# Hash attention and a gated feed-forward layer on one core: hash products, sums and casts placed anew

## The chip, the cores and the metric

The kernel runs on one core of a Trainium2 chip. The core has five engines, each with its own in-order queue of instructions: TensorE (PE, matrix products), VectorE (DVE), ScalarE (ACT), GpSimd (POOL) and SyncE (SP, which here issues transfers only). They wait for each other through semaphores. Transfers run on 16 DMA engines that all queues share. The metric is the time of one execution on the device in microseconds; the figure shown for a kernel is the median of several runs.

## The reference

Inputs are q, k and v of shape 4 batches x 8 heads x 768 tokens x 64, a random matrix `proj` of 64 x 6, and four weight matrices. All are float32.

```python
q_bits = (einsum('bhsd,dk->bhsk', q, proj) > 0)      # 6 bits, likewise k_bits
q_bucket = sum(q_bits * 2 ** arange(6))               # likewise k_bucket
scores = where(q_bucket == k_bucket, q @ k.T / 8, -1e9)
attn = softmax(scores) @ v
x = attn.transpose(0, 2, 1, 3).reshape(3072, 512)
ffn = (gelu(x @ w_gate) * (x @ w_val)) @ w_out         # d_ff = 1536
out = x + sigmoid(x @ w_res) * ffn
```

A token attends only to tokens of the same bucket, that is, to those whose six signs agree. The kernel does not build a mask: it appends the six bits (as plus or minus a half, with a constant) to the 64 values of q and k, scaled so that a score with unequal bits falls far below the others.

## The kernel before

Batches are numbered 0 to 3. A batch has 4 pairs of heads (pair p = 4 b + hp), each pair has 9 score chunks, so a batch has 36 slots; slot `s` of batch `b` is number `36 b + s` in the code. For every pair q and k must be brought into the form `aug`: cast to bf16 (`cast`, lines 259 to 263) into a tile `nat`, given their hash bits, and transposed, by a DMA transpose on SP (`turn`, line 359). There are four `nat` tiles, used in turn.

Each batch goes through three kinds of stage:

- Attention: in each slot TensorE computes one chunk of scores (line 499), ScalarE takes the exp (line 509), and two slots later TensorE multiplies with v (line 474). VectorE resets (`opened`, line 441), copies (`repeat`, line 453) and normalises (`finish`, lines 418 and 419) the accumulators `av`; there are two of them. The normalised rows are transposed into `x_sb` by SP (line 427). Between the chunks TensorE works off the second half of the feed-forward layer of the batch before (`project`, lines 555 and 569).
- Gate: for 12 steps m, TensorE multiplies x with a block of the gate weights and of the value weights (line 523), ScalarE takes the gelu of the first (line 540), VectorE multiplies the two (`hh`, line 543). Two PSUM tiles `sp` alternate, so the step after needs the gelu and the product of the step before.
- Project of the last batch, at the end.

The order of batch 0 and of its gate stage is written out by hand in `PLAN` and `BESIDE_GV`. For later batches, work is hung on slots with `at` and on gate steps with `gv`; what hangs on a slot or step is issued after its own work, in the order in which it was hung there.

The hash bits come about in two ways. For two pairs of a batch TensorE multiplies (line 282, ahead of gate step 1), and VectorE takes the signs in four small instructions for each of the four tiles (line 303, in gate steps 0, 1, 2 and 4). For the other two pairs of batches 2 and 3 (pairs 10, 11 and 14, 15) the work is spread out: for each of the four tiles there are 12 products of GpSimd (`product`, line 334), of half a tile with one column of `proj`, and 12 sums of VectorE over the 64 values (`add_up`, line 340). So batch b's attention, its gate stage and the attention of batch b + 1 together carry 48 products and 48 sums, for b = 1 and 2. `PLACES[b]` names the place of each product: `('a', b, s)` is slot s of batch b, `('g', b, m)` is gate step m. The products of attention slots use two buffers of the tag `gt`, which they share with the gelu's output; those of gate steps use two buffers of the tag `th`, shared with `project`. A product waits until its buffer is free, that is, until the sum two products before is done. Sums are not placed by themselves: `spread_out` issues one ahead of a product when two products are outstanding in its list, and the rest at a change of tag or at `DRAIN`. `LAYS` is where GpSimd turns the finished sums into bits (line 343) and SP transposes. `LDY` is where the tiles of these pairs are loaded, `CSY` at which gate step and on which engine they are cast; `LDX`, `TRX` and `CSX` are the first slots of the loads, VectorE's transposes (line 271) and GpSimd's casts of the other two pairs.

`load_rows` (line 350) loads the 384 numbers of `proj` to all 128 partitions, with a transfer on GpSimd's queue, and `spread_rows` (line 354) reorders them into the tile that all products read. GpSimd also prepares v for each pair (`vals_s` and `vals_a`, lines 385 to 397, a block of six instructions).

SP's queue is in order too: a transfer or a transpose that waits for its data holds up all behind it.

Of the kernel before, what the change touches and what calls it, by code (L numbers as in the profile page):

```python
# [9 lines left out]
FP32 = mybir.dt.float32  # L10
# [45 lines left out]
    ('turn_dma', 3, 0),  # L56
# [27 lines left out]
    (1, 'tokens', (6, 7), True), (4, 'cast', 6, 0, 'p'), (5, 'cast', 6, 1, 'p'), (7, 'cast', 7, 0, 'p'),  # L84
    (6, 'cast', 7, 1, 'p'), (7, 'bits', 6, 0, 'v'), (7, 'turn_dma', 6, 0), (10, 'bits', 6, 1, 'v'),
    (10, 'turn_dma', 6, 1), (9, 'bits', 7, 0, 'v'), (9, 'turn_dma', 7, 0), (10, 'bits', 7, 1, 'v'),
    (10, 'turn_dma', 7, 1), (9, 'ps'),
]
XDMA = 2
XJOIN = (1, 2)  # L90
# [3 lines left out]
def kernel(  # L94
# [13 lines left out]
    B, H, S, D = q.shape  # L108
    NBITS = proj.shape[1]
    DMODEL = H * D  # L110
    DFF = moe_w_gate.shape[1]
    P = 128
# [9 lines left out]

    LDX, TRX, CSX = 9, 24, 25
    LDY = {1: [('a', 1, 0), ('a', 1, 0), ('a', 1, 2), ('a', 1, 3)], 2: [('a', 2, 0), ('a', 2, 1), ('a', 2, 16), ('a', 2, 17)]}
    CSY = [(5, 's'), (6, 's'), (7, 's'), (8, 's')]
    PLACES = {1: [('a', 1, 11), ('a', 1, 12), ('a', 1, 13), ('a', 1, 14), ('a', 1, 15), ('a', 1, 16), ('a', 1, 17), ('a', 1, 18), ('a', 1, 21), ('a', 1, 22), ('a', 1, 23), ('a', 1, 24), ('a', 1, 25), ('a', 1, 26), ('a', 1, 31), ('a', 1, 32), ('g', 1, 0), ('g', 1, 0), ('g', 1, 1), ('g', 1, 1), ('g', 1, 2), ('g', 1, 2), ('g', 1, 3), ('g', 1, 3), ('g', 1, 4), ('g', 1, 4), ('g', 1, 5), ('g', 1, 5), ('g', 1, 6), ('g', 1, 6), ('g', 1, 7), ('g', 1, 7), ('g', 1, 8), ('g', 1, 8), ('g', 1, 9), ('g', 1, 9), ('g', 1, 10), ('g', 1, 10), ('a', 2, 2), ('a', 2, 3), ('a', 2, 4), ('a', 2, 5), ('a', 2, 6), ('a', 2, 7), ('a', 2, 8), ('a', 2, 9), ('a', 2, 12), ('a', 2, 13)], 2: [('a', 2, 14), ('a', 2, 15), ('a', 2, 16), ('a', 2, 17), ('a', 2, 18), ('a', 2, 21), ('a', 2, 22), ('a', 2, 23), ('a', 2, 24), ('a', 2, 25), ('a', 2, 26), ('a', 2, 31), ('a', 2, 32), ('g', 2, 0), ('g', 2, 0), ('g', 2, 1), ('g', 2, 1), ('g', 2, 2), ('g', 2, 2), ('g', 2, 3), ('g', 2, 3), ('g', 2, 4), ('g', 2, 4), ('g', 2, 5), ('g', 2, 5), ('g', 2, 6), ('g', 2, 6), ('g', 2, 7), ('g', 2, 7), ('g', 2, 8), ('g', 2, 8), ('g', 2, 9), ('g', 2, 9), ('g', 2, 10), ('g', 2, 10), ('a', 3, 2), ('a', 3, 3), ('a', 3, 4), ('a', 3, 5), ('a', 3, 6), ('a', 3, 7), ('a', 3, 8), ('a', 3, 9), ('a', 3, 12), ('a', 3, 13), ('a', 3, 14), ('a', 3, 15), ('a', 3, 16)]}
    DRAIN = {1: ('a', 2, 15), 2: ('a', 3, 18)}
    LAYS = {1: [('g', 1, 6), ('g', 1, 7), ('g', 1, 11), ('a', 2, 16)], 2: [('g', 2, 6), ('g', 2, 7), ('a', 3, 5), ('a', 3, 19)]}  # L130
    NE = 9
    C = 2048.0
    ALPHA = C / np.sqrt(D)
# [6 lines left out]
    g_pool = ctx.enter_context(tc.tile_pool(name="gtmp", bufs=2))  # L140
# [126 lines left out]
    def tr(p, side, c0=0, c1=HT):  # L267
        if (p, side) not in t32:
            t32[p, side] = t32_pool.tile([P, HT, 2, 32], FP32, tag="t32", name="t32")
        sl = slice(c0, c1)  # L270
        nc.vector.transpose(t32[p, side][:, sl].rearrange("p c h n -> p (c h n)"),  # L271
                            raw[p, side][:, sl].rearrange("p c d -> p (c d)"))
# [56 lines left out]
    def product(x, n, tag):  # L329
        bit, hi = divmod(n, 2)  # L330
        if x not in sums:
            sums[x] = hh_pool.tile([P, HT, NBITS], FP32, tag=f"sums{x[0] % 2}{x[1]}", name="sums")
        pr = g_pool.tile([P, T, D], FP32, tag=tag, name="pr")
        nc.gpsimd.tensor_mul(pr, raw[x][:, hi * T:(hi + 1) * T],  # L334
                             projr[:, bit].unsqueeze(1).to_broadcast([P, T, D]))
        prods.append((x, bit, hi, pr))
# [5 lines left out]
    def bits_sums(x):  # L342
        nc.gpsimd.tensor_scalar(nat_of(x)[:, :, D:D + NBITS], sums.pop(x), 0.0, 0.5,
                                op0=ALU.is_gt, op1=ALU.subtract)

    rows = []

    def load_rows():
        rows.append(g_pool.tile([P, D, NBITS], FP32, tag="th", name="pr"))
        nc.gpsimd.dma_start(rows[0].rearrange("p d n -> p (d n)"),  # L350
                            proj.rearrange("d n -> (d n)").partition_broadcast(P))

# [3 lines left out]
    def turn(p, side):  # L356
        x = (p, side)
        ag = aug_pool.tile([P, HT, P], BF16, tag=f"aug{side}", name=f"aug{side}")
        nc.sync.dma_start_transpose(out=ag, in_=nat_of(x).rearrange("p c n -> p (c n)"))
        aug[x] = ag  # L360
# [94 lines left out]
    def x_turn(b, hp):  # L455
        pt = mm_ps.tile([P, T, P], BF16, tag="f" if b == 0 else "r", name="pt")
        for t in range(T):
            nc.tensor.transpose(pt[:, t, :], x_tok[b][:, hp, t, :], ident)
        if hp == HP - 1:
            nc.scalar.activation(x_sb[b][:, hp, 0:2], pt[:, 0:2], AF.Copy)  # L460
            nc.vector.tensor_copy(x_sb[b][:, hp, 2:T], pt[:, 2:T])
        else:
            nc.vector.tensor_copy(x_sb[b][:, hp], pt)
# [117 lines left out]
    NSLOT = HP * NCH  # L581
# [7 lines left out]
    def at(s, *pieces):  # L589
        side_work.setdefault(s, []).extend(pieces)  # L590
# [4 lines left out]
    def gv(b, m, *pieces):  # L595
        gv_work.setdefault((b, m), []).extend(pieces)

    def loads(s, *xs):
        for p, what in xs:
            at(s, (lambda p=p: load_v(p)) if what == "v" else  # L600
               (lambda p=p, w=what: load(p, "qk".index(w))))
# [15 lines left out]
    def tokens(ps, psum=False):  # L617
        hash_tok([(p, side) for p in ps for side in range(2)], psum)
# [4 lines left out]
    def put(where, b, i, *pieces):  # L623
        if where == "g":
            gv(b, i, *pieces)
        else:
            at(b * NSLOT + i, *pieces)

    def spread_out(ys, places, drain, lays):
        work = [(y, n) for y in ys for n in range(2 * NBITS)]  # L630
        assert len(places) == len(work)
        left, tagged = [], None
        for k, (where, b, i) in enumerate(places):
            tag = "th" if where == "g" else "gt"
            if tagged not in (None, tag):
                for _ in left:
                    put("a", b, 0 if tag == "gt" else NSLOT - 1, add_up)
                left = []
            tagged = tag
            if len(left) > 1:  # L640
                left.pop(0)
                put(where, b, i, add_up)
            y, n = work[k]
            put(where, b, i, lambda y=y, n=n, tag=tag: product(y, n, tag))
            left.append((y, n))
        for _ in left:
            put(*drain, add_up)
        for y, p in zip(ys, lays):
            put(*p, lambda y=y: bits_sums(y), lambda y=y: turn(*y))

    for b in range(B - 1):
        s0, p0 = b * NSLOT, (b + 1) * HP
        xs = [(p0 + i, side) for i in range(2) for side in range(2)]
        ys = [(p0 + 2 + i, side) for i in range(2) for side in range(2)]
        if b == 0:
            continue
        for j, x in enumerate(xs):
            loads(s0 + LDX + 3 * j, (x[0], "qk"[x[1]]))
            at(s0 + TRX + 2 * j, lambda x=x: tr(*x))
            at(s0 + CSX + 2 * j, lambda x=x: cast(*x, nc.gpsimd))  # L660
        gv(b, 0, lambda p0=p0: tokens((p0, p0 + 1), True))
        for m, x in zip((0, 1, 2, 4), xs):
            lay(b, m, x)
        for y, (where, bb, i) in zip(ys, LDY[b]):
            put(where, bb, i, lambda y=y: load(y[0], y[1]))
        for y, (m, eng) in zip(ys, CSY):
            gv(b, m, lambda y=y, eng=eng: cast(*y, ENG[eng]))
        spread_out(ys, PLACES[b], DRAIN[b], LAYS[b])
    for p in range(HP, NPAIR):
        if 9 * p - 8 >= NSLOT:  # L670
            at(9 * p - 8, lambda p=p: vals_s(p), lambda p=p: vals_a(p))
        if 9 * p - 20 >= NSLOT:
            loads(9 * p - 20, (p, "v"))
# [25 lines left out]
    def first_gv(i):  # L699
# [3 lines left out]
        S=score, V=value, fill=fill, tr=tr,  # L703
# [9 lines left out]
        turn_dma=turn,  # L713
        hash=lambda ps, i: hash_mm([(p, side) for p in ps for side in range(2)], (i % 2,), (i // 2,)),
        tokens=tokens, bits=lambda p, side, e: bits(p, side, [ENG[x] for x in e]),
        va=vals_a, vs=vals_s, finish=finish, open=opened, preset=preset, repeat=repeat,
        pr=load_rows, ps=spread_rows, w=load_w, load=load, load_v=load_v, xturn=lambda hp: x_turn(0, hp),
        gelu=gelu_table, gv=first_gv)

    for m, name, *args in BESIDE_GV:  # L720
# [7 lines left out]
    for s in range(NSLOT, LAST):  # L728
# [11 lines left out]
        if slot == NSLOT - 1:  # L740
            values(*pending.pop(0))
            ps = (HP * (b + 1), HP * (b + 1) + 1)
# [47 lines left out]
```

## Time and profile before

| | us |
|---|---|
| median of 3 runs | 342.61 (342.59 to 343.22) |
| profiled execution | 344.1 |
| its span | 342.3 |
| TensorE busy | 331.2 |
| VectorE busy | 215.4 |
| ScalarE busy | 214.2 |
| GpSimd busy | 176.6 |

The span runs from the first to the last instruction that the profiler records; the execution is a little longer. Stages by the profile's clock: attention of batch 0 to about 47 us, its gate stage to 82, attention of batch 1 to 124, gate to 161, batch 2 to 204 and 241, batch 3 to 283 and 318, the last project to the end. In rows of a timeline the columns are start, length, engine, line, operation, output and input, and in brackets the idle time of the engine before it with what ended that. A row with x2 or x4 merges neighbours. In the chain of work that ended last each row is start, length and what held the path.

### The profile page before, as it was taken

Reading aid. Unit: us, or ns where it says so; the run is one execution under the profiler, and the core shown is the slowest. Engines: PE = TensorE matmul, PEld = TensorE weight load, DVE = VectorE, ACT = ScalarE, POOL = GpSimd, SP = SyncE. Lnnn points to the kernel's source line nnn. Section 1 sums busy time; section 2 is a strip of 40 time slices with the busy share of each in tenths; the row PEclk is TensorE's granted clock in tenths of the full one; section 3 lists DMA queues with packets and bytes.
Section 4 is the critical chain, followed back from the end, with each engine's and each line's share of the span. In section 5 each row is a group of like instructions: output and inputs, shape, how many; then the busy total and the mean of one; then the engine's idle time right before and its main releaser. Section 6 shows DMA issues by size and latency. Waiting matters only on the chain.

```text
span 342.3 us, 7607 instructions
## 1 busy us (share of the span) xinstructions
PE 331.2 (97%) x2995; PEld 203.1 (59%) x3042; DVE 215.4 (63%) x454; ACT 214.2 (63%) x247; POOL 176.6 (52%) x264
## 2 busy tenths in 40 slices
PE   8999999999999999999999999999999999999995
PEld 6666665565666655555666565555566665566443
DVE  7977455655467958877577875887477444343333
ACT  4989962237999952355999881254999984223120
POOL 3798940282248942688799971677988100000000
PEclk9999999999999999999999999999999999999998
DMA  7999999999987324434656823624041450000012
GB/s 209 377 255 186 294 180 159 165 171 131 246 295 195 83 74 92 90 72 57 170 180 183 237 75 101 124 47 92 2 125 45 64 101 31 33 0 2 31 71 86
DMA packets 74388, 43.89 MB, mean 128 GB/s; under 512 B 52544, under 2 KB 71360, under 8 KB 74352
## 3 DMA queue, kind: packets, MB, share of 16 engines
q1 hardware_dynamic: 67872, 37.95, 46.5%
q0 software_dynamic: 6400, 5.44, 10.6%
q8 instruction: 24, 0.39, 0.5%
q14 instruction: 12, 0.10, 0.1%
q10 hardware_dynamic: 80, 0.00, 0.0%
HBM read 29.56 MB, written 6.29 MB: 105 GB/s over the span
## 4 chain that ended last, share of the span: by engine, by line
PE 77%; DVE 7%; POOL 6%; DMA 4%; issue 3%; ACT 1%; SPq 1%; DVEq 0%; POOLq 0%; ACTq 0%
PE sp L523 31%; PE fps L569 16%; PE sp L499 14%; PE av L474 8%; PE rps L555 6%; DVE hh L543 3%; PE hs L282 2%; DMA ldv<-in_v_dram 2%; DMA aug<-nat 2%; POOL pr L334 2%; DVE nat L303 2%; DVE sums L340 1%; POOL nat L303 1%; ACT ering L509 1%; POOL va L385 1%
## 5 line engine op out<-in xcount | busy, mean ns | idle before, releaser
L334 POOL TENSOR_TENSOR pr<-ld,projr 128x384 f32<-128x384 f32 x96 | 93.5, 997 | 57.1 <-DVE sums L340 34.3
L509 ACT ACTIVATE e<-sp 128x1024 bf16<-128x1024 f32 x108 | 109.1, 1027 | 8.5 <-PE sp L499 3.4
L540 ACT ACTIVATE gt<-sp 128x768 bf16<-128x768 f32 x48 | 38.9, 810 | 84.7 <-PE sp L523 81.0
L499 PE MATMUL sp<-aug,aug 71*128 71x256 bf16 (+1 forms) x384 | 85.9, 325 | 1.5 <-ACT ering L509 0.6
L569 PE MATMUL fps<-wo,hh 128*128 128x512 bf16 (+2 forms) x287 | 74.4, 361 | 1.3
L543 DVE TENSOR_TENSOR hh<-gt,sp 128x768 bf16<-128x768 bf16 x48 | 45.8, 954 | 42.7 <-PE sp L523 39.2
L523 PE MATMUL sp<-x_sb,wv 128*128 128x512 bf16 (+1 forms) x374 | 70.4, 324 | 2.0 <-DVE hh L543 1.5
L523 PE MATMUL sp<-x_sb,wg 128*128 128x512 bf16 (+1 forms) x377 | 70.6, 325 | 0.4
L340 DVE TENSOR_REDUCE sums<-pr 128x6 f32<-128x384 f32 x96 | 50.0, 541 | 11.8 <-POOL pr L334 11.2
L474 PEld LDWEIGHTS <-e 128*128 128x128 bf16 x864 | 40.2, 97 | 25.1
L523 PEld LDWEIGHTS <-wv 128*128 128x128 bf16 x384 | 37.5, 98 | 27.4 <-issue 2.7
L523 PEld LDWEIGHTS <-wg 128*128 128x128 bf16 x384 | 37.1, 98 | 25.7 <-issue 1.5
L474 PE MATMUL av<-va,e 128*128 128x65 bf16 x864 | 43.4, 193 | 0.2
L569 PEld LDWEIGHTS <-hh 128*128 128x128 bf16 x312 | 28.1, 97 | 21.7
L499 PEld LDWEIGHTS <-aug 71*128 71x128 bf16 x384 | 29.2, 97 | 12.9 <-issue 3.3
L509 ACT ACTIVATE ering<-sp 128x1024 bf16<-128x1024 f32 x36 | 34.3, 1030 | 2.6 <-PE sp L499 2.4
L572 DVE SCALAR_TENSOR_TENSOR fps<-th,fps 128x512 f32<-128x512 f32 (+2 forms) x26 | 17.0, 653 | 28.3 <-PE fps L569 28.3
L555 PE MATMUL rps<-wr,x_sb 128*128 128x512 bf16 x91 | 26.0, 379 | 0.2
L559 ACT ACTIVATE th<-rps 128x512 f32<-128x512 f32 x24 | 14.3, 594 | 18.5 <-PE rps L555 18.5
L271 DVE STREAM_TRANSPOSE t<-ld 128x768 f32<-128x768 f32 (+3 forms) x28 | 23.2, 846 | 3.4 <-PE hs L282 1.9
L453 DVE COPY av<-av 128x390 f32<-128x390 f32 x24 | 13.6, 566 | 13.6 <-PE av L449 13.6
L261 POOL TENSOR_SCALAR nat<-ld 128x768 bf16<-128x768 f32 (+1 forms) x12 | 9.6, 803 | 20.1 <-DMA aug<-nat 16.7
(72 smaller groups left out, 264.6 us busy)
## 6 DMA issues: line engine op xcount, KB each, us to landing
ldv<-in_v_dram SPq DMA_DIRECT2D x16, 384.0 KB, 4.7
out_dram<-o SPq DMA_DIRECT2D x23, 256.0 KB, 2.1
ld<-in_q_dram SPq DMA_DIRECT2D x15, 384.0 KB, 5.2
ld<-in_k_dram SPq DMA_DIRECT2D x15, 384.0 KB, 6.0
wg<-in_moe_w_gate_dram POOLq DMA_DIRECT2D x4, 384.0 KB, 6.5
wv<-in_moe_w_val_dram POOLq DMA_DIRECT2D x4, 384.0 KB, 8.9
wo<-in_moe_w_out_dram POOLq DMA_DIRECT2D x3, 512.0 KB, 6.9
wr<-in_moe_w_res_dram POOLq DMA_DIRECT2D x1, 512.0 KB, 13.8
```

The source lines that it names most:

```text
L271: nc.vector.transpose(t32[p, side][:, sl].rearrange("p c h n -> p (c h n)"), raw[p, side][:, sl].rearrange("p c d -> p (c d)"))
L334: nc.gpsimd.tensor_mul(pr, raw[x][:, hi * T:(hi + 1) * T], projr[:, bit].unsqueeze(1).to_broadcast([P, T, D]))
L340: nc.vector.reduce_sum(sums[x][:, hi * T:(hi + 1) * T, bit], pr, axis=mybir.AxisListType.X)
L474: nc.tensor.matmul(av[p, hi][:, qt, :], e[:, off:off + P], va[:, hi, jt, 0:D + 1], start=first, stop=(repeats(p, hi) and jt == T - 1), ski ...
L499: nc.tensor.matmul(sp[:, off:off + nq * P], ks[0:KA, hi * T + jt, :], qs[0:KA, hi * T + qt0:hi * T + qt0 + nq, :], start=True, stop=True)
L509: nc.scalar.activation(e, sp, AF.Exp, scale=float(ALPHA))
L523: nc.tensor.matmul(sp[:, c0:c1], w[:, kk, bass.ts(m, P)], xs[:, kk, c0:c1], start=(kk == 0), stop=(kk == KM - 1))
L540: nc.scalar.activation(gt, sp[:, 0:S], AF.Gelu)
L543: nc.vector.tensor_mul(hidden[b][:, m, :], gt, ps[1][:, 0:S])
L555: nc.tensor.matmul(rps, x_sb[b][:, kk, t, :], wr[:, kk, :], start=(kk == 0), stop=(kk == KM - 1))
L569: nc.tensor.matmul(fps[:, cs], hh[:, m, bass.ts(t, P)], wo[:, m, cs], start=(m == 0), stop=(m == KF - 1))
L572: nc.vector.scalar_tensor_tensor(fps[:, cs], th[:, cs], 1.0, fps[:, cs], op0=ALU.add, op1=ALU.mult)
```

## The change

Nothing is computed otherwise, and no instruction is added or left out. The lists of places are new, and the load and the spread of `proj` move from the hand-written plan of batch 0 to slots 1 and 8 of batch 1; the load's buffer has the tag `gt` in place of `th`. All code below line 131 stands one line lower in the new kernel (from line 669 on, three).

```diff
-    ('S', 20), ('pr',), ('tr', 5, 1), ('load', 6, 0), ('V', 17),
+    ('S', 20), ('tr', 5, 1), ('load', 6, 0), ('V', 17),
...
-    (10, 'turn_dma', 7, 1), (9, 'ps'),
+    (10, 'turn_dma', 7, 1),
...
-    LDX, TRX, CSX = 9, 24, 25
-    LDY = {1: [('a', 1, 0), ('a', 1, 0), ('a', 1, 2), ('a', 1, 3)], 2: [('a', 2, 0), ('a', 2, 1), ('a', 2, 16), ('a', 2, 17)]}
-    CSY = [(5, 's'), (6, 's'), (7, 's'), (8, 's')]
...
-    DRAIN = {1: ('a', 2, 15), 2: ('a', 3, 18)}
-    LAYS = {1: [('g', 1, 6), ('g', 1, 7), ('g', 1, 11), ('a', 2, 16)], 2: [('g', 2, 6), ('g', 2, 7), ('a', 3, 5), ('a', 3, 19)]}
+    LDX, TRX, CSX = 9, 26, 26
+    LDY = {1: [('a', 1, 0), ('a', 1, 0), ('a', 1, 3), ('a', 1, 1)], 2: [('a', 2, 0), ('a', 2, 2), ('a', 2, 19), ('a', 2, 19)]}
+    CSY = [(5, 's'), (5, 's'), (10, 's'), (10, 's')]
...
+    DRAIN = {1: ('a', 2, 16), 2: ('a', 3, 20)}
+    LAYS = {1: [('g', 1, 7), ('g', 1, 8), ('a', 2, 5), ('a', 2, 17)], 2: [('g', 2, 7), ('g', 2, 8), ('a', 3, 6), ('a', 3, 21)]}
+    PRS = (1, 8)
...
-        rows.append(g_pool.tile([P, D, NBITS], FP32, tag="th", name="pr"))
+        rows.append(g_pool.tile([P, D, NBITS], FP32, tag="gt", name="pr"))
...
+    at(NSLOT + PRS[0], load_rows)
+    at(NSLOT + PRS[1], spread_rows)
```

The places of the 48 products of each list, as slots of a batch's attention or steps of its gate stage (5x2 means two products at 5):

| list | where | before | after |
|---|---|---|---|
| 1 | attention 1 | 11 to 18, 21 to 26, 31, 32 (16) | 9, 10x2, 11, 13, 15x2, 16, 17, 18x2, 21 to 24, 26, 27, 30, 34 (19) |
| 1 | gate 1 | 0 to 10, two each (22) | 0x3, 1, 2, 3x2, 4, 5x2 to 10x2, 11 (21) |
| 1 | attention 2 | 2 to 9, 12, 13 (10) | 2, 3, 5, 6, 8, 9, 13, 14 (8) |
| 2 | attention 2 | 14 to 18, 21 to 26, 31, 32 (13) | 1, 2, 13, 14, 16, 18, 19, 23, 24x2, 26, 31 to 33 (14) |
| 2 | gate 2 | 0 to 10, two each (22) | 0x4, 1, 2, 3x2, 4, 5x2, 6x2, 7, 8x2 to 10x2 (20) |
| 2 | attention 3 | 2 to 9, 12 to 16 (13) | 0, 4x3, 6 to 8, 13x2 to 15x2, 16 (14) |

In the order that results, a gate step with the four bit instructions has two sums behind them before (steps 1, 2 and 4) and one after. Both lists are under way in attention 2 at once after the change: products of pair 11 and of pair 14 alternate in slots 1 to 14, on the same two buffers.

More of the change, by code (lines that the diff above doesn't have):

```diff
@@ L121 @@
     assert D == 64 and S == 768 and 4 * NBITS <= 32 and HP == KM
-    LDX, TRX, CSX = 9, 24, 25
-    LDY = {1: [('a', 1, 0), ('a', 1, 0), ('a', 1, 2), ('a', 1, 3)], 2: [('a', 2, 0), ('a', 2, 1), ('a', 2, 16), ('a', 2, 17)]}
-    CSY = [(5, 's'), (6, 's'), (7, 's'), (8, 's')]
-    PLACES = {1: [('a', 1, 11), ('a', 1, 12), ('a', 1, 13), ('a', 1, 14), ('a', 1, 15), ('a', 1, 16), ('a', 1, 17), ('a', 1, 18), ('a', 1, 21), ('a', 1, 22), ('a', 1, 23), ('a', 1, 24), ('a', 1, 25), ('a', 1, 26), ('a', 1, 31), ('a', 1, 32), ('g', 1, 0), ('g', 1, 0), ('g', 1, 1), ('g', 1, 1), ('g', 1, 2), ('g', 1, 2), ('g', 1, 3), ('g', 1, 3), ('g', 1, 4), ('g', 1, 4), ('g', 1, 5), ('g', 1, 5), ('g', 1, 6), ('g', 1, 6), ('g', 1, 7), ('g', 1, 7), ('g', 1, 8), ('g', 1, 8), ('g', 1, 9), ('g', 1, 9), ('g', 1, 10), ('g', 1, 10), ('a', 2, 2), ('a', 2, 3), ('a', 2, 4), ('a', 2, 5), ('a', 2, 6), ('a', 2, 7), ('a', 2, 8), ('a', 2, 9), ('a', 2, 12), ('a', 2, 13)], 2: [('a', 2, 14), ('a', 2, 15), ('a', 2, 16), ('a', 2, 17), ('a', 2, 18), ('a', 2, 21), ('a', 2, 22), ('a', 2, 23), ('a', 2, 24), ('a', 2, 25), ('a', 2, 26), ('a', 2, 31), ('a', 2, 32), ('g', 2, 0), ('g', 2, 0), ('g', 2, 1), ('g', 2, 1), ('g', 2, 2), ('g', 2, 2), ('g', 2, 3), ('g', 2, 3), ('g', 2, 4), ('g', 2, 4), ('g', 2, 5), ('g', 2, 5), ('g', 2, 6), ('g', 2, 6), ('g', 2, 7), ('g', 2, 7), ('g', 2, 8), ('g', 2, 8), ('g', 2, 9), ('g', 2, 9), ('g', 2, 10), ('g', 2, 10), ('a', 3, 2), ('a', 3, 3), ('a', 3, 4), ('a', 3, 5), ('a', 3, 6), ('a', 3, 7), ('a', 3, 8), ('a', 3, 9), ('a', 3, 12), ('a', 3, 13), ('a', 3, 14), ('a', 3, 15), ('a', 3, 16)]}
@@ L129 @@
-    DRAIN = {1: ('a', 2, 15), 2: ('a', 3, 18)}
-    LAYS = {1: [('g', 1, 6), ('g', 1, 7), ('g', 1, 11), ('a', 2, 16)], 2: [('g', 2, 6), ('g', 2, 7), ('a', 3, 5), ('a', 3, 19)]}
+    LDX, TRX, CSX = 9, 26, 26
+    LDY = {1: [('a', 1, 0), ('a', 1, 0), ('a', 1, 3), ('a', 1, 1)], 2: [('a', 2, 0), ('a', 2, 2), ('a', 2, 19), ('a', 2, 19)]}
+    CSY = [(5, 's'), (5, 's'), (10, 's'), (10, 's')]
+    PLACES = {1: [('a', 1, 9), ('a', 1, 10), ('a', 1, 10), ('a', 1, 11), ('a', 1, 13), ('a', 1, 15), ('a', 1, 15), ('a', 1, 16), ('a', 1, 17), ('a', 1, 18), ('a', 1, 18), ('a', 1, 21), ('a', 1, 22), ('a', 1, 23), ('a', 1, 24), ('a', 1, 26), ('a', 1, 27), ('a', 1, 30), ('a', 1, 34), ('g', 1, 0), ('g', 1, 0), ('g', 1, 0), ('g', 1, 1), ('g', 1, 2), ('g', 1, 3), ('g', 1, 3), ('g', 1, 4), ('g', 1, 5), ('g', 1, 5), ('g', 1, 6), ('g', 1, 6), ('g', 1, 7), ('g', 1, 7), ('g', 1, 8), ('g', 1, 8), ('g', 1, 9), ('g', 1, 9), ('g', 1, 10), ('g', 1, 10), ('g', 1, 11), ('a', 2, 2), ('a', 2, 3), ('a', 2, 5), ('a', 2, 6), ('a', 2, 8), ('a', 2, 9), ('a', 2, 13), ('a', 2, 14)], 2: [('a', 2, 1), ('a', 2, 2), ('a', 2, 13), ('a', 2, 14), ('a', 2, 16), ('a', 2, 18), ('a', 2, 19), ('a', 2, 23), ('a', 2, 24), ('a', 2, 24), ('a', 2, 26), ('a', 2, 31), ('a', 2, 32), ('a', 2, 33), ('g', 2, 0), ('g', 2, 0), ('g', 2, 0), ('g', 2, 0), ('g', 2, 1), ('g', 2, 2), ('g', 2, 3), ('g', 2, 3), ('g', 2, 4), ('g', 2, 5), ('g', 2, 5), ('g', 2, 6), ('g', 2, 6), ('g', 2, 7), ('g', 2, 8), ('g', 2, 8), ('g', 2, 9), ('g', 2, 9), ('g', 2, 10), ('g', 2, 10), ('a', 3, 0), ('a', 3, 4), ('a', 3, 4), ('a', 3, 4), ('a', 3, 6), ('a', 3, 7), ('a', 3, 8), ('a', 3, 13), ('a', 3, 13), ('a', 3, 14), ('a', 3, 14), ('a', 3, 15), ('a', 3, 15), ('a', 3, 16)]}
@@ L716 @@
         va=vals_a, vs=vals_s, finish=finish, open=opened, preset=preset, repeat=repeat,
-        pr=load_rows, ps=spread_rows, w=load_w, load=load, load_v=load_v, xturn=lambda hp: x_turn(0, hp),
+        w=load_w, load=load, load_v=load_v, xturn=lambda hp: x_turn(0, hp),
         gelu=gelu_table, gv=first_gv)
```

## The prediction

> **What bounds the kernel now.** I read the page first, then the busy time by stage, then the chain that ended last inside the gate stages, then each engine's timeline where the change bites. "Batch 1" and so on count from 0; a "slot" is one score chunk of 36 per batch.
>
> ```profile
> PE 331.2 (97%) x2995; PEld 203.1 (59%) x3042; DVE 215.4 (63%) x454; ACT 214.2 (63%) x247; POOL 176.6 (52%) x264
> ```
>
> TensorE is busy 97% of the span, so only places where it runs slower than it could are worth anything. By stage (from:to, length, then PE, PEld, DVE, ACT, POOL busy):
>
> ```profile
> 124.00:161.00 37.00, 36.04 (x236) 20.89 (x237) 27.42 (x54) 15.40 (x20) 21.91 (x24) 1.00 0.44 84
> 204.00:241.00 37.00, 35.99 (x234) 20.88 (x237) 27.53 (x54) 15.27 (x19) 21.99 (x24) 1.00 0.41 84
> 283.00:318.00 35.00, 34.79 (x213) 20.59 (x214) 13.53 (x17) 12.05 (x16) 0.00 (x0) 1.00 0.04 16
> ```
>
> The gate stages of batches 1 and 2 leave TensorE about 1 us idle each, that of batch 3, which has no hash work, 0.2. The chain there (start, us, what) names who held it, and the same stretch in batch 2:
>
> ```profile
> 135.13 0.59 DVE sums L340 x2
> ...
> 136.18 0.95 DVE hh L543
> ...
> 144.82 0.97 DVE hh L543
> ```
> ```profile
> 224.74 0.97 DVE hh L543
> ```
>
> VectorE's own timeline gives the terms of a step m, and in brackets what it waited for (batch 1, then the first row of batch 2):
>
> ```profile
> 133.17 0.95 DVE L543 TENSOR_TENSOR hh<-gt,sp 128x768 bf16<-128x768 bf16 x1 [1.03 <-PE sp L523]
> 134.16 0.95 DVE L303 TENSOR_SCALAR nat<-htp 32x72 bf16<-32x72 f32 x4
> 135.13 1.01 DVE L340 TENSOR_REDUCE sums<-pr 128x6 f32<-128x384 f32 x2
> ...
> 150.00 0.95 DVE L543 TENSOR_TENSOR hh<-gt,sp 128x768 bf16<-128x768 bf16 x1 [0.72 <-PE sp L523]
> ...
> 152.60 0.95 DVE L543 TENSOR_TENSOR hh<-gt,sp 128x768 bf16<-128x768 bf16 x1 [0.72 <-PE sp L523]
> ```
> ```profile
> 213.09 0.95 DVE L543 TENSOR_TENSOR hh<-gt,sp 128x768 bf16<-128x768 bf16 x1 [1.18 <-PE sp L523]
> ```
>
> Where VectorE waits for TensorE, hh follows hh every 2.60 us (150.00 to 152.60): TensorE's own pace. Where a step also carries four hash-bit instructions and two sums, it is 0.99 + 0.97 + 1.05 = 3.01 us (133.17, 134.16, 135.13, 136.18), and TensorE waits for VectorE. Over four steps that is 144.82 - 133.17 = 11.65 against 4 x 2.60 = 10.40: 1.25 us lost, and again 11.65 from 213.09 to 224.74.
>
> **The change, part by part.** No instruction is added or dropped: 96 products, 96 sums, 8 ScalarE casts, one rows load and its spread stand elsewhere.
>
> *Sums in the gate stages.* The new placement puts one sum behind m = 0 (two in batch 2), one each in m = 1, 2 and 4, where the bits are, and two where there are none. A step with bits is then 0.99 + 0.97 + 0.50 = 2.46 us, below 2.60. Both stages gain 1.25: **-2.5 us**. Bounds: 2.5 if the pace is TensorE's throughout, 0 if something else holds 3.0. I take the whole, since m = 5 onwards runs two sums at 2.60 already. The sums behind m = 0 are hidden by VectorE's wait for TensorE ahead of m = 1: 0.50 in a gap of 1.03, and 1.01 in one of 1.18; without that gap each would delay hh by its length.
>
> *ScalarE's casts*, two in m = 5 and two in m = 10 in place of one each in 5 to 8:
>
> ```profile
> 143.00 0.81 ACT L540 ACTIVATE gt<-sp 128x768 bf16<-128x768 f32 x1 [2.21 <-PE sp L523]
> 143.71 0.83 ACT L259 ACTIVATE nat<-ld 128x768 bf16<-128x768 f32 x1
> ```
>
> Two casts end at 143.00 + 0.71 + 2 x 0.83 = 145.37, the next gelu is due at 145.60: 0, hidden by the wait for TensorE with 0.2 us to spare; without that cover each late 0.1 us would delay hh by as much.
>
> *Rows load out of batch 0.* It is issued by GpSimd at the moment that the last transposes of batch 0 start, and TensorE waits for one of these:
>
> ```profile
> 36.86 0.60 PE L499 MATMUL sp<-aug,aug 71*128 71x512 bf16 x2 [0.52 <-DMA aug<-nat]
> ```
> ```profile
> pr<-in_proj_dram POOLq DMA_DIRECT2D x1, 192.0 KB, 4.5
> ```
>
> Between 0 and -0.52; nothing is added there. I take **-0.3**. ScalarE's exps are the next thing late.
>
> *Rows load into batch 1.* It now waits for the gelu buffer that hh of m = 10 frees at the end of batch 0's gate stage, and the spread waits for its landing, 4.5 us. GpSimd sat idle there until the first q tile landed, and the 11.93 us hold the landing, the spread and one value block (2.87, below), so this by itself costs 0; with less idle time it would move the first product one to one:
>
> ```profile
> 91.40 1.95 POOL L334 TENSOR_TENSOR pr<-ld,projr 128x384 f32<-128x384 f32 x2 [11.93 <-DMA ld<-in_q_dram]
> 95.03 1.00 POOL L334 TENSOR_TENSOR pr<-ld,projr 128x384 f32<-128x384 f32 x1 [1.68 <-DVE sums L340]
> ...
> 120.62 1.95 POOL L334 TENSOR_TENSOR pr<-ld,projr 128x384 f32<-128x384 f32 x2
> ```
>
> *GpSimd through the attention stage of batch 1.* Behind the third product (about 94.9, when the first sum frees its buffer) there now stand, ahead of the gate stage, 16 more products (before: 13), three blocks of value preparation (before: two, the other ran in the idle time ahead of 91.40) and four casts. Prices from one stretch of its timeline:
>
> ```profile
> 185.22 1.00 POOL L393 TENSOR_TENSOR v<-ldv 128x384 f32<-128x384 f32 x1
> ...
> 188.09 2.91 POOL L334 TENSOR_TENSOR pr<-ld,projr 128x384 f32<-128x384 f32 x3
> ...
> 192.74 0.83 POOL L261 TENSOR_SCALAR nat<-ld 128x768 bf16<-128x768 f32 x1
> ```
>
> 17 x 0.97 + 3 x 2.87 + 4 x 0.80 = 28.3 us, so the last product ends at 94.9 + 28.3 = 123.2, where before it ended at 122.6. It has no gap left. Its sum stands on VectorE ahead of the last projection step and the last x_tok, whose transpose TensorE needs to open the gate stage:
>
> ```profile
> 125.21 1.21 SPq L427 DMA_TRANSPOSE x_sb<-x_tok  x1
> ```
> ```profile
> DMA to landing us min/median/max: 2.7/2.7/2.7
> ```
> ```profile
> 128.27 0.65 PE sp L523 x4
> ```
>
> 125.21 + 2.7 = 127.9: 0.35 us to spare, and 0.6 is asked. One more place ahead of it is tight. The sum of the twelfth product ends at 94.9 + 9 x 0.97 + 2 x 2.87 + 1.00 + 0.54 = 110.9, and behind it on VectorE stand x_tok, one more sum and an av reset, which TensorE wants at
>
> ```profile
> 112.11 0.19 PE L449 MATMUL av<-vsum,eps_sb 128*128 128x65 bf16 x1
> ```
>
> I estimate that it comes at 112.2. Together 0.3 if the load of q lands when it did; every 0.1 us that it is later adds 0.1. That load is issued behind three transposes which share the DMA engines with the rows' 192 KB:
>
> ```profile
> 77.72 9.26 SPq L359 DMA_TRANSPOSE aug<-nat  x3
> 87.03 1.29 SPq L161 DMA_DIRECT2D ld<-in_q_dram  x1
> ```
>
> Bounds: 0 and, if the transposes ran at half rate for the rows' 4.5 us, +2.25. The q load is issued after the transposes in any case, so I stay near the lower end and add 0.3: **+0.6** in all. The Trainium skill, "DMA: Bandwidth & Descriptors", section "Queues, rings and completion order", speaks against this edit: each DMA engine alternates between the queues that have work, packet by packet. By that rule alone the load would cost its half share, +2.25, and the sum would be -0.2; no row of this profile shows the two together.
>
> *Batch 2's attention.* Before, one av reset came late because its chain ran through GpSimd:
>
> ```profile
> 188.18 0.92 POOL pr L334
> ...
> 191.70 0.12 DVE av L441
> ...
> 191.87 0.20 PE av L449
> ```
>
> In the new order the sum that VectorE waited for there (its product ended at 189.1) has its product one wait earlier, so the reset is ready in time. I take **-0.25**, an estimate above the 0.17 that the reset itself shows (191.70 to 191.87); bounds -0.4 and, if the two interleaved lists (four products outstanding on two buffers) make VectorE wait ahead of an av copy, +0.4.
>
> *Batch 3's attention.* The last pair's k bits move from slot 19 to 21, which puts them behind a value block on GpSimd, and their transpose behind an output DMA on SP:
>
> ```profile
> 265.46 0.82 POOL L385 CAST va<-ldv 128x768 bf16<-128x768 f32 x1
> ```
> ```profile
> 263.48 1.44 SPq L359 DMA_TRANSPOSE aug<-nat  x1
> 266.50 0.34 SPq L577 DMA_DIRECT2D out_dram<-o  x1
> ```
> ```profile
> 271.04 0.60 PE L499 MATMUL sp<-aug,aug 71*128 71x512 bf16 x2
> ```
>
> Bits at 266.2, issue at 266.9, needed at 271.04. Landing took 4.9 us there, 3.7 for its twin in batch 2, 8.5 among the weight loads:
>
> ```profile
> DMA to landing us min/median/max: 4.9/4.9/4.9
> ```
> ```profile
> DMA to landing us min/median/max: 3.7/3.7/3.7
> ```
> ```profile
> DMA to landing us min/median/max: 8.5/8.5/8.5
> ```
>
> So the wait is 0 (3.7), 0.76 (4.9) or 4.4 us (8.5). I take **+0.3**, between the two near rows.
>
> Edits at nothing: the swapped k and q loads, and transposes and casts two slots later, are through with the GpSimd chain's 123.2 above, and the hash matmuls that need them stand behind the row at 128.27; without that cover each would be paid in full at the gate's start.
>
> Sum: -2.5 - 0.3 + 0.6 - 0.25 + 0.3 = **-2.15 us**. The profiled span of 342.3 becomes 340.15; the 1.8 us around the span (344.1 in all) stay. That execution stood 1.5 above the median of 342.61, so I carry the difference over: **340.5**.
>
> **The rivals.** A, the sum above: 340.5, by its terms' near bounds 339.6 to 341.6.
>
> B, the rows load holds up the q load by more: speaking for it, the saturated transposes and a GpSimd chain with no gap; against it, that the rows' 4.5 us begin before the last two transposes and end early in them. At 1.5 us later, 1.2 more than in A: 341.7. From about 1.5 us more it is no longer a measurable gain.
>
> C, slower: the transpose of the last pair's k lands as late as 8.5 us, with no other work for TensorE. -2.15 - 0.3 + 4.4 = +1.9: 344.5. It decides from a landing of 6.6 us (266.9 + 6.6 = 271.04 + 2.45). For it: the slack that there was (263.48 + 4.9 = 268.4 against 271.04) is spent wholly. Against: 8.5 was seen only next to weight loads, which are over by then.
>
> D, the change does not do what it says: steps m = 1, 2, 4 stay at 3.0 us, because a sum waits for its product now that each buffer is freed later. The rest remains: -0.3 + 0.6 - 0.25 + 0.3 = +0.35, 343.0. Against it: a product takes 0.97 and is issued a step ahead.
>
> **How the numbers follow.** Chances: A 0.56, B 0.15, C 0.17, D 0.12. Less than 0.2% (0.7 us) is about what a measurement of this kernel cannot tell from no change. Faster: A nearly whole (0.54), two thirds of B (0.10), a little of C (0.03), 0.67. Within: the rest of A and B and most of D, 0.15. Slower: 0.18. The range is 339.4 to 343.4: A with its bounds, B and D, leaving out most of C and the ends; the likeliest case alone is 339.6 to 341.6.
>
> **What would show it.** Right: hh every 2.60 us from m = 1 to m = 5 in batches 1 and 2; the wait of 0.52 gone from batch 0; GpSimd without a gap from 95 to 123 us. Wrong: steps of 3.0 left in a gate stage (D); the first product well after 91.4 (B); TensorE waiting several us for aug at the last pair of batch 2 or 3 (C); or a wait for a sum in front of an av copy in batch 2, which the sum prices at nothing.

## The result, and the profile after

| | before | after |
|---|---|---|
| median, us | 342.71 (342.21 to 343.36, 9 runs) | 340.75 (339.64 to 341.56, 9 runs) |
| ratio to before | | 0.9938 (95%: 0.9923 to 0.9954) |
| profiled execution, and its span, us | 344.1, 342.3 | 340.08, 338.4 |

The change makes the kernel 1.96 us faster (by the ratio's interval 1.6 to 2.6); 2.1 were forecast (340.5 against 342.61). Three runs of the experiments below, one of the rows' load alone and two of the rows loaded twice, had a mean granted TensorE clock of 0.990 to 0.993 in place of 0.997 to 1.000, and took 346.2 to 346.9 us. The profiled pair is 3.9 us apart in span. To see what of this belongs to the change, the span is cut at TensorE's first score of batches 1, 2 and 3 and at its last projection. These are the rows of its timeline, first before, then after:

```profile
80.50 0.60 PE L499 MATMUL sp<-aug,aug 71*128 71x512 bf16 x2
...
160.13 0.60 PE L499 MATMUL sp<-aug,aug 71*128 71x512 bf16 x2
...
240.05 0.60 PE L499 MATMUL sp<-aug,aug 71*128 71x512 bf16 x2
...
335.30 2.81 PE L569 MATMUL fps<-wo,hh 128*128 128x256 bf16 x36
```
```profile
79.72 0.60 PE L500 MATMUL sp<-aug,aug 71*128 71x512 bf16 x2
...
158.38 0.60 PE L500 MATMUL sp<-aug,aug 71*128 71x512 bf16 x2
...
236.90 0.60 PE L500 MATMUL sp<-aug,aug 71*128 71x512 bf16 x2
...
332.26 2.81 PE L570 MATMUL fps<-wo,hh 128*128 128x256 bf16 x36
```

The differences of these rows, and of the same rows of every later profile (us; "batch 1" is its attention and its gate stage; the experiments are told below):

| kernel | batch 0 | batch 1 | batch 2 | batch 3 | rest of span |
|---|---|---|---|---|---|
| before | 80.50 | 79.63 | 79.92 | 95.25 | 7.0 |
| before, again | 79.63 | 79.63 | 79.92 | 95.25 | 7.0 |
| after | 79.72 | 78.66 | 78.52 | 95.36 | 6.1 |
| after, again | 79.27 | 78.72 | 78.52 | 95.39 | 6.7 |
| places of the gate stages alone | 79.69 | 78.41 | 78.86 | 95.26 | 7.2 |
| rows' load alone | 79.73 | 79.63 | 79.96 | 95.25 | 7.0 |
| three casts in m = 5 | 80.12 | 78.79 | 78.58 | 95.38 | 6.7 |
| two products moved | 79.46 | 78.48 | 78.22 | 95.38 | 6.6 |
| and hash bits of batch 0 | 79.63 | 78.29 | 78.21 | 95.39 | 6.9 |
| and three sums behind resets | 79.51 | 78.22 | 78.22 | 95.25 | 6.9 |
| rows loaded twice | 81.47 | 79.64 | 79.95 | 95.26 | 6.6 |

In the two kernels that were profiled twice the three columns in the middle repeat to 0.06 us; batch 0 and the tail differ by up to 0.9 and 0.6. So the change is worth -0.97, -1.40 and +0.11 in batches 1 to 3, -2.26 in all. The other 0.78 (batch 0) and 0.86 (tail) of the profiled pair are of the size of that scatter (over all profiles the tail lies between 6.1 and 7.2): the second pair shows 0.36 and 0.3 there.

The gate stages by the busy time of the engines, the same stretches as before:

```profile
124.00:161.00 37.00, 36.74 (x240) 21.41 (x243) 27.34 (x54) 16.22 (x21) 20.77 (x23) 1.00 0.52 106
204.00:241.00 37.00, 36.74 (x246) 21.59 (x250) 27.04 (x53) 17.01 (x21) 22.32 (x27) 1.00 0.40 79
283.00:318.00 35.00, 34.79 (x203) 20.14 (x206) 13.08 (x16) 10.32 (x13) 0.00 (x0) 1.00 0.03 8
```

TensorE now idles 0.26 us in each of the first two, as little as in the stage without hash work. VectorE's timeline in batch 1 shows why:

```profile
132.65 0.95 DVE L544 TENSOR_TENSOR hh<-gt,sp 128x768 bf16<-128x768 bf16 x1 [0.59 <-PE sp L524]
133.63 0.94 DVE L304 TENSOR_SCALAR nat<-htp 32x72 bf16<-32x72 f32 x4
134.61 0.56 DVE L341 TENSOR_REDUCE sums<-pr 128x6 f32<-128x384 f32 x1
135.25 0.95 DVE L544 TENSOR_TENSOR hh<-gt,sp 128x768 bf16<-128x768 bf16 x1
...
158.65 0.95 DVE L544 TENSOR_TENSOR hh<-gt,sp 128x768 bf16<-128x768 bf16 x1 [0.72 <-PE sp L524]
```

The last hh of the same stage before:

```profile
160.40 0.95 DVE L543 TENSOR_TENSOR hh<-gt,sp 128x768 bf16<-128x768 bf16 x1 [0.72 <-PE sp L523]
```

hh follows hh at 2.60 us with one group of bits and one sum between. From m = 1 to m = 11 it takes 158.65 - 132.65 = 26.00, ten times 2.60, where before it took 160.40 - 133.17 = 27.23.

Two waits of the new kernel stand in the chain that ended last. The first is the opening of batch 1's gate stage, the second the opening of batch 2:

```profile
121.20 0.97 POOL pr L335
...
124.21 0.57 DVE x_tok L420
...
124.80 2.75 DMA x_sb<-x_tok
...
127.59 0.81 PE sp L524 x4
...
158.65 0.95 DVE hh L544
159.60 0.94 DVE sums L341 x2
...
160.62 0.60 ACT th L560
161.22 0.92 ACT e L510
162.14 0.04 issue
162.19 0.59 PE sp L500 x2
```

GpSimd runs without a gap from 94.11 to 122.2, as the prediction reckoned. Its last product of the stage is late, so is the sum behind it on VectorE, the last x_tok and its transpose. And the tanh of `project` needs a `th` buffer that a product behind m = 11 has filled: it waits for that sum, and the exp that TensorE needs stands behind the tanh on ScalarE.

### The profile page after: what moved, and what is told of

The parts are those of the page before. It is cut to its first block, busy times and chain, and to the rows that moved or that the text cites. A ratio compares the mean times of both kernels' runs of the same rounds, so it can differ in the third digit from the quotient of the medians.

```text
span 338.4 us, 7607 instructions
## 1 busy us (share of the span) xinstructions
PE 330.2 (98%) x2995; PEld 203.2 (60%) x3042; DVE 215.4 (64%) x454; ACT 214.3 (63%) x247; POOL 176.6 (52%) x264
## 4 chain that ended last, share of the span: by engine, by line
PE 81%; POOL 8%; ACT 5%; DVE 3%; issue 2%; DMA 1%; POOLq 0%; DVEq 0%; ACTq 0%
PE sp L524 36%; PE fps L570 14%; PE sp L500 13%; PE av L475 7%; PE rps L556 5%; ACT ering L510 5%; POOL pr L335 4%; PE hs L283 3%; PE wps L228 1%; PE hs L318 1%; POOL v L394 1%; PE pt L373 1%; DMA x_sb<-x_tok 1%; DVE sums L341 1%; POOL va L386 1%
## 5 line engine op out<-in xcount | busy, mean ns | idle before, releaser
L335 POOL TENSOR_TENSOR pr<-ld,projr 128x384 f32<-128x384 f32 x96 | 93.8, 998 | 47.8 <-DVE sums L341 31.6
```

The lines of the kernel that those rows point to most:

```text
L335: nc.gpsimd.tensor_mul(pr, raw[x][:, hi * T:(hi + 1) * T], projr[:, bit].unsqueeze(1).to_broadcast([P, T, D]))
```

## The experiments

**The places of the gate stages alone**, in the kernel before (shown for batch 1, batch 2 likewise; one product of each list goes into the next attention stage, and with it, in list 1, the bits of the third tile move from gate step 11 to slot 1 of batch 2):

```diff
-('g',1,0) x2, ('g',1,1) x2, ('g',1,2) x2, ('g',1,3) x2, ('g',1,4) x2, ...
+('g',1,0) x4, ('g',1,1), ('g',1,2), ('g',1,3) x2, ('g',1,4), ...
```

> The kernel before, with nothing changed but the places of products and sums in the gate stages of batches 1 and 2: two sums behind m = 0, one each in m = 1, 2 and 4, two elsewhere (one product of each list goes into the next attention stage instead). Theory of the prediction: hh follows hh every 2.60 us from m = 1 to m = 5 in both stages, 1.25 us gained in each, and nothing given back: 2.5 us below the kernel before, about 340.2. Rival (D): something else holds the steps at 3.0, no gain, 342.7. A third way: the steps go to 2.60, and part comes back in the attention stage that follows, between the two.

Measured 340.98 us beside 343.29 before, ratio 0.9929 (0.9916 to 0.9943): 2.31 us faster. Every step from m = 1 on takes 2.60 in both stages:

```profile
132.37 0.96 DVE L543 TENSOR_TENSOR hh<-gt,sp 128x768 bf16<-128x768 bf16 x1
...
134.97 0.95 DVE L543 TENSOR_TENSOR hh<-gt,sp 128x768 bf16<-128x768 bf16 x1
```

The table has -1.22 in batch 1 and -1.06 in batch 2, whose attention pays some of it back. The thinner steps by themselves give the whole gain of the change; D falls.

**The rows' load alone**, in the kernel before:

```diff
-('S', 20), ('pr',), ...          (9, 'ps'),       tag="th"
+at(NSLOT + 1, load_rows); at(NSLOT + 8, spread_rows)   tag="gt"
```

> The kernel before, with the load of the random rows and its spread moved from batch 0 to slots 1 and 8 of batch 1, nothing else. Theory of the prediction: the wait of 0.52 us for aug in batch 0 goes, wholly or in part, and batch 1 pays nothing: 0.3 to 0.5 us below the kernel before, 342.2 to 342.4. Rival (B, and the half share of the DMA queues): the rows' 4.5 us hold up the last transposes and with them the q load, so that the first product of batch 1 starts up to 2.25 us later than 91.40. Second rival, from the trace of the changed kernel: the spread's 0.87 us no longer stand on GpSimd ahead of the last weight load, so that load, the transposes and the q load all come earlier, and the first product starts 1.5 to 2.5 us before 91.40.

Measured 342.64 us beside 343.29, ratio 0.9992 (0.9971 to 1.0014): not to be told from no change. Without the one of the twelve runs that was named above (346.86) the means are 0.6 us apart (0.2 to 1.0), which would fit the theory, but to leave it out is a choice made after the fact. Batch 1 takes 79.63 as before, so there the load costs nothing. The first product starts at 89.24, earlier than 91.40, as the second rival had it. The q load is issued at 83.75 to 84.7 in three profiles of the changed order of GpSimd and in this one, but at 87.29 in the run with two products moved, which is the changed kernel up to there. The eleven profiles agree with the rival all the same. Where GpSimd issues the last weight load 8.4 us or more ahead of batch 1's first score, as in these four (in this run at 71.34 against 79.73), the q load is issued 4.4 to 4.8 us behind that score; where it comes 6.2 to 7.8 us ahead, as in the seven others, the q load is issued 6.5 to 7.8 us behind. The run with two products moved belongs to the second group: its weight load is at 72.76, after GpSimd had paused for 4.94 us without a reason in the profile, where the eight other profiles with batch 0's hash bits in their old places have 3.06 to 3.30. That the weight load is the cause is not shown; no run moves it alone.

**The rows loaded twice in batch 0**, in the kernel before (the second copy is not used):

```diff
+more = g_pool.tile([P, D, NBITS], FP32, tag="th", name="pr2")
+# the same dma_start into `more`
```

> The kernel before, with the 192 KB of random rows loaded twice in batch 0 (the second copy is not used). Theory of the prediction: the rows' transfer is what makes TensorE wait for aug in batch 0; another 4.5 us of transfer beside the same transposes makes that wait 1 to 2.8 us (0.52 plus between a small and a half share of 4.5 us), 0.5 to 2.3 us above the kernel before. Rival: the wait of 0.52 comes from how the transposes fall in an execution and not from the rows: 0 to 0.6 us of wait as without the second copy, and the time is that of the kernel before.

Measured 345.44 us beside 342.81, ratio 1.0081 (1.0052 to 1.0110): 2.6 us slower at the median, above the 0.5 to 2.3 expected. Two of the four are the runs named above (346.22 and 346.56); the other two took 344.66 and 343.84, 1.0 to 1.9 us above the kernel before. TensorE's wait for aug, here and in the second profile of the kernel before:

```profile
35.22 0.59 PE L501 MATMUL sp<-aug,aug 71*128 71x512 bf16 x3
...
37.83 0.60 PE L501 MATMUL sp<-aug,aug 71*128 71x512 bf16 x2 [1.60 <-DMA aug<-nat]
```
```profile
34.88 0.59 PE L499 MATMUL sp<-aug,aug 71*128 71x512 bf16 x3
...
36.00 0.61 PE L499 MATMUL sp<-aug,aug 71*128 71x512 bf16 x2
```

The distance of the two scores is 0.92 us without a wait (35.10 to 36.02 in the changed kernel). With the rows once it is 1.53 in the first profile of before, 1.12 in the second and 0.92 in the run of the places alone; with the rows twice 2.61. The transposed tile that TensorE waits for landed 6.9 us after its issue with the rows twice, and after 4.9 to 5.8 with the rows once. So a transfer can delay the transposes, as the prediction's theory has it, and the wait of 0.52 was more than usual. But the rows are not its only cause: in the run of three casts, which has no rows' load there, the tile landed after 5.4 us and the distance is 1.11 (35.37 to 36.48), as in the second profile of before. Without the rows the landings are 3.9 to 5.4, which overlaps with the rows once.

**The kernel before, once more**:

> The kernel before once more, for a second profile. If the 0.52 us wait for aug in batch 0 belongs to the kernel, it is there again; if it differs between executions, it is gone or of another length, and the first hh comes at 50.2 to 50.9 us instead of 51.27. From the last hh of one gate stage to the last of the next: 79.20, 79.92 and 77.12 us again.

One run, 343.1 us. The wait is there with 0.2 in place of 0.6 us (the distance of the two scores beyond 0.92), and the three middle columns of the table are those of the first profile.

**The changed kernel, once more**:

> The changed kernel unchanged, beside the next runs on the same chip. If the earlier comparison holds: 2.0 us below the kernel before (1.5 to 2.6). By the stages of its profile, counted from the last hh of one gate stage to the last hh of the next: batch 1 78.2, batch 2 78.5, batch 3 77.2 us, as in the first profile of it; what differs between executions lies in batch 0, in the transposes behind it and at the tail.

Measured 340.57 us beside 342.81, ratio 0.9936 (0.9925 to 0.9948), and the columns of the table within 0.06.

**Three casts in m = 5**, in the changed kernel:

```diff
-CSY = [(5, 's'), (5, 's'), (10, 's'), (10, 's')]
+CSY = [(5, 's'), (5, 's'), (5, 's'), (10, 's')]
```

> The changed kernel with three of ScalarE's casts in m = 5 (one in m = 10) in batches 1 and 2. Three casts end at 143.00 + 0.71 + 3 x 0.83 = 146.20 in the clock of the profile before, 0.6 us after the next gelu is due. Theory of the prediction: the gelu has no slack, each late 0.1 us delays hh by as much: 0.6 us in each of two stages, 1.2 us above the changed kernel, 341.95. Rival: a late gelu costs nothing until it ends after the value matmuls of its step, 1.30 - 0.81 = 0.49 us of slack; then hh is late by 0.1 in each stage, 0.2 us in all, 340.95.

Measured 341.04 us beside 343.29, ratio 0.9942 (0.9925 to 0.9958). ScalarE's and VectorE's timelines:

```profile
142.16 0.81 ACT L541 ACTIVATE gt<-sp 128x768 bf16<-128x768 f32 x1 [1.79 <-PE sp L524]
142.87 2.30 ACT L260 ACTIVATE nat<-ld 128x768 bf16<-128x768 f32 x3
145.07 0.80 ACT L541 ACTIVATE gt<-sp 128x768 bf16<-128x768 f32 x1
```
```profile
146.13 0.95 DVE L544 TENSOR_TENSOR hh<-gt,sp 128x768 bf16<-128x768 bf16 x1 [0.72 <-PE sp L524]
...
148.78 0.95 DVE L544 TENSOR_TENSOR hh<-gt,sp 128x768 bf16<-128x768 bf16 x1 [0.78 <-PE sp L524]
```

The three casts take 2.30 us, less than the 2.49 reckoned. The gelu starts 145.07 - 142.16 = 2.91 behind the one before it, 0.31 late where 0.6 was expected, and the hh of its own step is on time (146.13). Only one step later does hh come after 2.65 in place of 2.60. The table has 0.07 to 0.13 us in batch 1 and 0.06 in batch 2, hardly more than executions differ. The rival was right that there is slack; that the two stages pay 1.2 us was wrong.

**Two products moved**, in the changed kernel:

```diff
-('a',1,30), ('a',1,34), ('g',1,0) x3, ...   ('g',1,10) x2, ('g',1,11), ('a',2,2)
+('a',1,30), ('g',1,0) x4, ...               ('g',1,10) x2, ('a',2,1), ('a',2,2)
```

> The changed kernel with two products moved: the last of batch 1's attention (slot 34) goes to step m = 0 of the gate stage, and the one behind m = 11 goes to slot 1 of batch 2. Theory: the x_sb transpose of batch 1 waits no more behind a sum that waits for GpSimd (0.26 us), and the tanh that opens batch 2 no longer waits for the sums that hold its buffer (0.31 us): 0.57 us below the changed kernel, 340.2. Rival: either wait is replaced by the next one in line (the x_sb transpose's own landing, ScalarE's table load), and the gain is 0 to 0.3.

Measured 340.14 us beside 343.29, ratio 0.9910 (0.9895 to 0.9924). Against the changed kernel batch 1 falls by 0.18 to 0.24 and batch 2 by 0.30. The tanh has no wait left:

```profile
158.96 1.02 ACT L510 ACTIVATE e<-sp 128x1024 bf16<-128x1024 f32 x1
159.88 0.59 ACT L560 ACTIVATE th<-rps 128x512 f32<-128x512 f32 x1
```

This execution also tries rival B. GpSimd's timeline shows the rows landing late, and with them the q load, 3 us later than in the first profile of the changed kernel:

```profile
78.39 0.56 POOL L351 DMA_DIRECT2D pr<-in_proj_dram  x1 [4.83 <-DVE hh L544]
...
86.71 0.86 POOL L355 COPY projr<-pr 128x384 f32<-128x384 f32 x1 [4.77 <-DMA pr<-in_proj_dram]
91.78 3.08 POOL L335 TENSOR_TENSOR pr<-ld,projr 128x384 f32<-128x384 f32 x3 [4.21 <-DMA ld<-in_q_dram]
```
```profile
88.89 1.95 POOL L335 TENSOR_TENSOR pr<-ld,projr 128x384 f32<-128x384 f32 x2 [4.78 <-DMA ld<-in_q_dram]
94.11 1.00 POOL L335 TENSOR_TENSOR pr<-ld,projr 128x384 f32<-128x384 f32 x1 [3.26 <-DVE sums L341]
```

Yet the third product starts at about 93.8 (91.78 + 2 x 1.0), no later than the 94.11 of the second fence, and batch 1 is the shorter of the two. The third product waits for a sum, and that stands on VectorE behind an x_tok, whatever the q load does (the changed kernel's VectorE; in the run with two products moved these two start at 92.76 and 93.23):

```profile
93.01 0.56 DVE L420 TENSOR_TENSOR x_tok<-av,rec 128x384 bf16<-128x384 f32 x1
93.48 1.00 DVE L341 TENSOR_REDUCE sums<-pr 128x6 f32<-128x384 f32 x2
```

The two later runs that keep the two moves have the q load late as well (86.70 and 87.34), so whether the lateness belongs to the execution or to these kernels is open.

**Hash bits of batch 0**, on top of the two moves, in a stage that the change did not touch:

```diff
-(2, 'bits', 4, 0, 'v'), (2, 'turn_dma', 4, 0),   (10, 'bits', 6, 1, 'v'), (10, 'turn_dma', 6, 1),
+(0, 'bits', 4, 0, 'v'), (0, 'turn_dma', 4, 0),   (8, 'bits', 6, 1, 'v'), (8, 'turn_dma', 6, 1),
```

> The changed kernel with the two moved products of the run before, and in the gate stage of batch 0, which the change did not touch, one group of four hash-bit instructions moved from m = 2 to m = 0 and one from m = 10 to m = 8, so that no step carries two groups. Theory (a step of the gate stage takes VectorE's 0.99 + 0.24 for each hash-bit instruction, or TensorE's 2.60, whichever is longer): the steps of 2.81 + 2.57 become 5.20 and the step of 3.03 becomes 2.60, 0.61 us; with the two moves 0.5 more: 339.6 if the changed kernel is at 340.7. Rival: batch 0's gate stage is held by the transposes and weight loads that run there, and the steps only change places: 340.2.

Measured 340.01 us beside 342.81, ratio 0.9916 (0.9901 to 0.9931). The rule of the step holds: two groups of bits were 2 x 1.0 + 1.0 = 3.0 us, one is 2.0, and all steps from m = 1 on are 2.60 now, as the last two hh show:

```profile
77.30 0.95 DVE L544 TENSOR_TENSOR hh<-gt,sp 128x768 bf16<-128x768 bf16 x1 [0.60 <-PE sp L524]
78.29 1.04 DVE L304 TENSOR_SCALAR nat<-htp 32x72 bf16<-32x72 f32 x4
79.90 0.95 DVE L544 TENSOR_TENSOR hh<-gt,sp 128x768 bf16<-128x768 bf16 x1 [0.57 <-PE sp L524]
```

From the first hh to the last it takes 79.90 - 50.57 = 29.33, where the changed kernel took 29.93. But of these 0.60 TensorE gains 0.37: 0.18 up to its first score of batch 1 (29.06 from the first hh on, 29.24 before the move) and 0.19 after it. The late last hh was partly hidden, since the first score of batch 1 does not need it. The whole time does not show the gain: the ratio was 0.9910 without this move and is 0.9916 with it.

**Three sums behind resets**, on top of that:

```diff
-('a',1,23), ('a',1,24), ('a',1,26)     ('a',3,14), ('a',3,15), ('a',3,15), ('a',3,16)
+('a',1,23), ('a',1,25), ('a',1,26)     ('a',3,14), ('a',3,16), ('a',3,16), ('a',3,17)
```

> The run with the moved hash bits, and in it one sum of batch 1 and two of batch 3 placed behind, not ahead of, the reset of an av tile on VectorE. Theory: these sums wait for GpSimd's products, and the resets that stand behind them reach TensorE 0.07 us late in batch 1 and 0.1 us late in batch 3; from the first score of one batch to that of the next, batch 1 falls from 78.3 to 78.2 us, and from the first score of batch 3 to the last projection it falls from 95.39 to 95.27, the 95.25 of the kernel before. Rival: the 0.1 us of batch 3 belongs to the k transpose of the last pair, moved two slots later, and stays: 95.39. In the time of the whole, 0.17 us is within the scatter: 340.0 less 0 to 0.4.

Measured 339.79 us beside 343.11, ratio 0.9898 (0.9883 to 0.9912), the lowest median of all, though its interval overlaps that of the two moves alone. Batch 1 is 78.22 and batch 3 is 95.25: both resets were what the sums delayed, and batch 3's 0.11 did not belong to the transpose. From the score to the `av` matmul that needs the reset, it takes 0.44 in place of 0.50 in batch 1, and in batch 3 0.43, where the changed kernel took 0.53. In the changed kernel the reset of batch 3 stands behind a sum that GpSimd holds up:

```profile
257.40 0.56 DVE L341 TENSOR_REDUCE sums<-pr 128x6 f32<-128x384 f32 x1 [0.20 <-POOL pr L335]
257.97 0.11 DVE L442 MEMSET av<- 128x65 f32 x1
```

## Why the prediction came out right, point by point

- **Sums in the gate stages, -2.5: right.** 27.23 - 26.00 = 1.23 us in each stage, -2.46, and the run with nothing else changed gives 2.31.
- **Casts, 0: right, for a wrong reason.** There were not 0.2 us of cover but more, since hh also needs the value matmuls, which end later than the gelu. A gelu 0.31 late cost 0.05 a step, so "each late 0.1 us would delay hh by as much" is refuted.
- **Rows out of batch 0, -0.3: neither refuted nor shown.** Batch 0 took 80.50, 79.63 and 79.69 in the profiles with the rows there, and 79.72, 79.27, 79.73, 80.12 and 79.46 without: means 0.28 apart, with a scatter of 0.9. That a transfer beside the transposes can delay aug is shown by the doubled load; that the rows once are worth 0.3 is not, and the run of three casts has a wait of 0.2 without them.
- **Batch 1, +0.6: too high; +0.26** (-0.97 + 1.23). The wait of x_sb (0.18 to 0.24) and the av reset (0.07) came as described. The step that failed is the 0.3 for the q load, twice over. In the changed kernel the load was issued not later than before but earlier, at 84.12 in place of 87.03 (2.1 us earlier, counted from batch 1's first score). And "every 0.1 us that it is later adds 0.1" overlooked that the third product waits for a place on VectorE: with the rows moved alone batch 1 paid 0.00, and a q load 3 us later paid nothing either. The Trainium skill, "DMA: Bandwidth & Descriptors", section "Queues, rings and completion order", lets the queues share each DMA engine packet by packet. An estimate by that rule: another 4.5 us of rows would hold up transposes by a half share, 2.25. With the rows twice aug came 1.1 to 1.7 us later, which fits a sharing below that half; the prediction's "no row of this profile shows the two together" holds for batch 1 only, since its own wait of 0.52 in batch 0 is such a row. The time of batch 1 hung on something else.
- **Batch 2, -0.25: -0.17** (-1.40 + 1.23), made up otherwise. The reset gave 0.32: from the score to the `av` matmul that needs it, it took 0.75 before and 0.43 after (rows below). Another 0.15 came at the gate's opening, where the hh of m = 1 follows the first by 3.45 in place of 3.60; the first x_sb matmul there no longer starts late, and I take it that x_tok, 0.2 earlier, is the cause; no run isolates it. Against that stands a step that the prediction left out: the product behind m = 11 makes the tanh wait, 0.31 us, shown by moving it (0.30). The feared wait ahead of an av copy did not come: from score to score, all other slots of the stage are as before to 0.03 us.

```profile
191.12 0.60 PE L499 MATMUL sp<-aug,aug 71*128 71x512 bf16 x2
191.87 0.20 PE L449 MATMUL av<-vsum,eps_sb 128*128 128x65 bf16 x1
```
```profile
189.68 0.60 PE L500 MATMUL sp<-aug,aug 71*128 71x512 bf16 x2
190.11 0.19 PE L450 MATMUL av<-vsum,eps_sb 128*128 128x65 bf16 x1
```

- **Batch 3, +0.3: +0.11, from another place.** The k transpose was issued at 263.89, landed after 3.8 us and was needed at 268.01: nothing. The 0.11 was an av reset.

```profile
263.89 1.47 SPq L360 DMA_TRANSPOSE aug<-nat  x1
```
```profile
aug<-nat SPq DMA_TRANSPOSE x1, 3.8
```
```profile
268.01 0.60 PE L500 MATMUL sp<-aug,aug 71*128 71x512 bf16 x2
```

So the large term was right and decided the case. The three small terms that the spans measure were off by 0.1 to 0.35, and their errors did not cancel: the forecast for batches 1 to 3 was -2.5 + 0.6 - 0.25 + 0.3 = -1.85, and -2.46 + 0.26 - 0.17 + 0.11 = -2.26 came. The forecast total of -2.15 lies near the -1.96 and -2.24 of the two comparisons because it also counts -0.3 for batch 0, which these medians do not show. That the total came so close is partly luck; the intervals would hold -2.56, the spans' -2.26 with the -0.3, as well. Carrying over the 1.5 us by which the profiled execution stood above the median was right in kind: 0.9 of it lay in batch 0, the only column in which the second profile of before (343.1 in all) is shorter.

## What to carry to other kernels

Where two engines take turns on two buffers, add up per step what each must issue; in these stages work placed in a step was free up to the longer sum and cost in full beyond it, except at the last step, so thin the steps that are already laden. Before counting a late transfer, look at what its user waits for next: if a place in another engine's order comes later, the transfer has slack. And when a placement moves work to the border of two stages, list who takes the shared buffers next, here the tanh behind a sum; such waits of 0.1 to 0.3 us were found by cutting the span at fixed instructions, where it repeated to 0.06 us while the whole time scattered by 1 to 2.

## What was not expected of the hardware

The same instructions ahead of the same point took different times on the DMA side: the q load of batch 1 was issued at 84.12 and 83.75 us in the two profiles of the changed kernel and at 87.29 in the run that differs from it only later, and there the rows' 192 KB took 8.3 us from issue to use of the landing (78.39 to 86.71), 4.6 in the changed kernel (78.65 to 83.24). Part of it began earlier, with GpSimd's unexplained pause of 4.94 us ahead of its last weight loads. The tail behind the last projection took between 6.1 and 7.2 us. Both exceed the smaller terms of the forecast.
